# Attention with a gated feed-forward: when GpSimd forms the down-weight sums, who scales the query weights, and the order of the first gate/up products

## The chip, the cores and the metric

One core of a Trainium2 chip runs the whole program. The metric is the device time of one execution in microseconds (us); lower is better. The engines are TensorE (PE in the profile, PEld for its weight loads), VectorE (DVE), ScalarE (ACT), GpSimd (POOL) and SyncE (SP, which here only issues DMAs). Each engine works through its own instructions in the order in which the program issued them, and waits on semaphores.

## The reference, cut to what matters

```python
xn   = layernorm(x)                                   # x: 2048 x 512
q    = xn @ wq                                        # 32 heads of 128
s    = (softmax(q k_cache^T / sqrt(128)) v_cache) @ wo    # 2048 keys, every head
gate = xn @ W_gate ; up = xn @ W_up                   # 512 -> 1792
g    = silu((relu(gate) * up) @ W_down)               # 1792 -> 512
out  = x + s * g
```

All inputs are bfloat16. There is no mask.

## The kernel before

The 2048 rows are four blocks of 512, Q0 to Q3. The program has three stages that matter here.

**Head.** Q0 goes through gate and up in the usual way (14 chunks of 128 hidden columns) and then through the down product `emit_down`: four tiles j = 0 to 3 of 128 rows, each 14 matmuls into one PSUM bank. Behind each tile ACT takes a tanh into `sig_sb`, and DVE makes two operations (lines 866 and 870) that write the gate `g_sb`. Between the tiles the program inserts other work. DVE builds the sums of transposed rows `TX` (kept in the buffer `xn_sb`) and `TZ` (lines 642 to 665) that the next stage reads, and POOL builds the weight sums `SG` of chunks 0 and 1 (`gu_sums`, lines 684 to 689). The sums of chunk 0 lie in the buffer `PT`, those of chunk 1 in `SG`, at the same address as the second tanh buffer.

**The 768-column pass.** Gate and up of Q1, Q2 and Q3 are done as a 2 by 2 block product with seven products instead of eight, m = 1 to 7. Each product is four matmuls (two of 512 and two of 256 columns), all at line 1236. One chunk k of 14 has its seven products, `emit_gu(k, m)`, in the order 1, 2, 6, 5, 7, 4, 3, woven between two chunks by the step number 7k + off[m]. Results are carried by copies of ACT (line 1247) and additions of DVE (lines 1190 and 1243), all of which read PSUM. DVE then multiplies gate by up from SBUF operands alone: line 1180 (512 columns, into `hT`) and line 1181 (256 columns, into a small buffer in `PT` that a DMA saves). `gside(t, ...)` hangs other work on step t. At the end of the pass the first three score pairs of attention and one query product step are woven in.

**Attention.** 128 blocks (head, Q) of eight pairs each. A pair is two score matmuls (line 1705), one exponential of ACT (line 1723) and eight value matmuls (line 1820). The PSUM banks for scores and all other products are a ring of three slots of two banks; PE waits for the oldest slot to be read. Tables say after which pair of which block (block, pair) other work is issued: `at(...)` for PE products and `side` for the rest. So the query projection of the next heads (`emit_st`, line 940 on PE, lines 945 and 954 on DVE), and the down product of Q1, Q3 and Q2 as seven products `emit_d` (line 1320, then lines 1329 to 1360 on DVE) run between pairs. For Q1, `emit_d` runs m = 1, 2, 6, 5, 7, 3, 4 at (0,2), (1,5), (2,5), (3,4), (4,5), (5,0) and (5,5). It needs sums of `hT` (`emit_hs`, DVE, lines 818 to 827) and sums of the down weights (`emit_wd_sums`, four POOL operations of 1792 columns, lines 794 to 800): m = 6 waits for the second of them, m = 7 for the third, m = 4 for the fourth.

In this kernel `emit_wd_sums` is listed at pairs (0,0) to (0,3), and then POOL scales the query weights of heads 2 and 3 (line 707) and forms their sums (`emit_sw(1)`). POOL's order alone decides when they start: the sums wait only for the scaled weights, which ACT has ready by then.

Three waits matter below, in `gu_sums`, in `emit_wd_sums` and in `emit_S_tile`, where the exponential of pair 3 waits for the last of lines 1180 and 1181:

```python
if k == 1:
    _wait(pool, sem_g.cur())
...
if k == 0:
    _wait_all(pool, [wd_tok["scale"], sem_nm.cur()])
...
if gp == NPB - 3:
    _wait(act, sem_hp.cur())
```

Of the kernel before, what the change touches and what calls it, by code (L numbers as in the profile page):

```python
# [6 lines left out]
F32 = mybir.dt.float32  # L7
F16 = mybir.dt.float16
ALU = mybir.AluOpType
# [43 lines left out]
def bass_recurrent_scan__mha_block_cached__glu_gated_reglu__prompt_kernel(  # L53
# [22 lines left out]
    FC = F // 128  # L76
# [40 lines left out]
    with ExitStack() as es:  # L117
# [60 lines left out]
        gr_sb = [at_(96256 + 1024 * i, [128, NQ], BF16, "gr_sb") for i in range(NSLOT)]  # L178
        sig_sb = [at_(99328 + 2048 * i, [128, D], F32, "sig_sb") for i in range(2)]
        small = [103424]  # L180
# [496 lines left out]
        def gu_sums(k):  # L677
            W, X = w_chunk(k), SG[k % 2]
            _wait_all(pool, [gu_tok[(k, "s")], gu_tok.get((k - 2, 7))])
            if k == 1:  # L680
                _wait(pool, sem_g.cur())
            a11, a12 = W[:, 0, 0:HC, :], W[:, 0, HC:DC, :]
            a21, a22 = W[:, 1, 0:HC, :], W[:, 1, HC:DC, :]
            k1 = sem_sg.sig(pool.tensor_tensor(X[:, 0], a21, a22, ALU.add))
# [9 lines left out]
        sw_tok = {}  # L694

        def emit_sw(pr):
            b = pr % 2
            W = Wq_sb[b]
            _wait(pool, wq_tok(pr))
            if pr >= 3:  # L700
                _wait(pool, qp_done_tok[pr - 2])
            wflat = W[:].rearrange("p c i e -> p (c i e)")
            if pr == 0:
                _wait(act, wq_tok(pr))
                k = sem_tws.sig(act.activation(wflat, wflat, ACTF.Copy, scale=WSC))
            else:
                k = sem_sw.sig(pool.tensor_scalar(wflat, wflat, WSC, None, op0=ALU.mult))  # L707
# [5 lines left out]
            if pr == 1:  # L713
                _wait(pool, sem_gup.cur())
            k1 = sem_sw.sig(pool.tensor_tensor(X[:, 0], a21, a22, ALU.add))
# [69 lines left out]
        def emit_wd_sums(k):  # L785
# [48 lines left out]
        def emit_down(h_last_tok, between):  # L834
            ytok = None
            for j in range(4):
# [27 lines left out]
                _wait(dve, stok)  # L864
                ttok = sem_g.sig(
                    dve.tensor_scalar(sig_sb[jb][:], sig_sb[jb][:], 1.0, r2[:, j, 0:1],
                                      op0=ALU.add, op1=ALU.mult))
                _wait(dve, ttok)
                gtok = sem_g.sig(
                    dve.tensor_tensor(g_sb[:, n, :], sig_sb[jb][:], yps, ALU.mult))  # L870
                sig_free[jb] = gtok
                if j < 2:
                    acc_free[jb] = gtok
                else:
                    ring_tok[s] = ring_tok[s] + [gtok]
                y_last["t"] = ytok
# [325 lines left out]
        def emit_gu(k, m):  # L1202
# [953 lines left out]
        def gu_begin():  # L2156
            gpool[:] = [s_ for s_ in ring_order if s_ != ring_order[-1]] + [NSLOT, ring_order[-1]]

# [6 lines left out]
        def gu_run(a, b):  # L2165
# [129 lines left out]
```

## Time and profile before

| | us |
|---|---|
| three runs of the kernel before | 1251.51, 1250.81, 1251.87 |
| their median | 1251.51 |
| the profiled execution | 1250.87 |
| its span in the trace | 1249.6 |
| PE busy in the span | 1218.5 |
| ACT, DVE, POOL busy | 1075.5, 864.1, 783.4 |

Times in the trace count from the start of the span; about 1.3 us of the profiled execution lie outside it. In the rows of the timeline the first column is the start in us and the second the duration (where a row stands for several instructions, from the start of the first to the end of the last). Then come the engine, the line in the source, the operation, what is written and read, and the shapes. In brackets stands how long the engine was idle ahead of the instruction and who ended that. The head ends and the 768-column pass begins near 41 us; the pass ends near 127 us, where the first pairs of attention are already under way.

### The profile page before, as it was taken

To read this page: it belongs to the slowest core of one execution; us is meant where nothing else is said; L and a number is where in the kernel's file an instruction comes from. 1 tells how busy PE (TensorE), PEld (TensorE's weight loads), DVE (VectorE), ACT (ScalarE), POOL (GpSimd) and SP (SyncE) were. 2 spreads that over 40 slices of the span, in tenths; PEclk is the share of its full clock that TensorE was granted. 3 is DMA by queue.
4 is the path that set the end of the run, shared out by engine and by line. 5 is a ranking of instruction groups with operands and counts; after the bars stand their busy time and mean duration, and the time that the engine had idled before them with its cause. 6 is when DMAs were issued, how large, how long until landed. Compare 5 with 4: busy or idle time off the path is not lost.

```text
span 1249.6 us, 29220 instructions
## 1 busy us (share of the span) xinstructions
PE 1218.5 (98%) x11798; PEld 825.1 (66%) x12010; DVE 864.1 (69%) x1304; ACT 1075.5 (86%) x1154; POOL 783.4 (63%) x904
## 2 busy tenths in 40 slices
PE   9996999999999999999999999999999999999998
PEld 5453677776666666666666666666666666666665
DVE  6899635546667776667666776677766766676587
ACT  7684777878899999999999999999999999999994
POOL 3557010013567767887768867886788776758367
PEclk9997999999999999999999999999999999999999
DMA  9500144115222445237533664347522762348616
GB/s 286 98 30 22 31 90 106 31 39 127 56 52 47 94 114 165 36 64 195 172 70 52 174 161 119 52 98 178 174 36 60 186 190 52 52 102 156 128 37 138
DMA packets 273719, 127.23 MB, mean 102 GB/s; under 512 B 238768, under 2 KB 268208, under 8 KB 268720
## 3 DMA queue, kind: packets, MB, share of 16 engines
q1 hardware_dynamic: 272240, 124.55, 42.7%
q8 instruction: 96, 1.57, 0.5%
q10 hardware_dynamic: 1344, 0.79, 0.2%
q14 instruction: 39, 0.32, 0.1%
HBM read 56.10 MB, written 27.00 MB: 67 GB/s over the span
## 4 chain that ended last, share of the span: by engine, by line
PE 94%; issue 2%; DVE 2%; POOL 1%; ACT 1%; DVEq 0%; POOLq 0%; ACTq 0%
PE ps_acc L1820 37%; PE ps_r L1705 34%; PE ps_r L1076 5%; PE ps_r L1602 3%; PE ps_r L1236 3%; PE ps_r L1320 3%; PE ps_r L940 2%; PE ps_r L1537 2%; PE ps_r L773 2%; PE ps_acc L1236 1%; DVE PT L1181 1%; PE ps_r L1634 1%; PE ps_r L1633 1%; PE ps_r L855 0%; PE ps_acc L855 0%
## 5 line engine op out<-in xcount | busy, mean ns | idle before, releaser
L1723 ACT ACTIVATE PT<-ps_r 128x1024 bf16<-128x1024 f32 x1024 | 987.8, 1025 | 119.4 <-PE ps_r L1705 101.8
L1820 PEld LDWEIGHTS ps_acc<-V_sb,PT 128*128 128x128 bf16 x8192 | 547.1, 98 | 223.5 <-issue 31.0
L1820 PE MATMUL ps_acc<-V_sb,PT 128*128 128x129 bf16 x8192 | 635.6, 220 | 1.1
L1705 PE MATMUL ps_r<-QT_sb,KT_sb 128*128 128x512 bf16 x1851 | 578.6, 380 | 15.4 <-DVE gu L1243 4.4
L1081 DVE TENSOR_TENSOR UVR<-UVR,ps_r 128x512 f32<-128x512 f32 (+1 forms) x228 | 168.9, 756 | 96.7 <-PE ps_r L1076 91.9
L1705 PEld LDWEIGHTS ps_r<-QT_sb,KT_sb 128*128 128x128 bf16 x2048 | 160.5, 98 | 42.3 <-ACT PT L1723 33.8
L1468 DVE TENSOR_TENSOR s_acc<-s_acc,ps_r 128x1024 f32<-128x1024 f32 x108 | 131.5, 1220 | 27.3 <-PE ps_r L1537 19.4
L1484 DVE TENSOR_TENSOR s_acc<-s_acc,ps_r 128x512 f32<-128x512 f32 x152 | 101.0, 683 | 28.9 <-PE ps_r L1602 23.5
L1743 DVE TENSOR_TENSOR Onorm<-ps_acc,rz_sb 128x512 bf16<-128x512 f32 x127 | 87.8, 691 | 4.4
L1568 POOL TENSOR_TENSOR TI<-OX 128x512 f16<-128x512 f16 x38 | 43.1, 1156 | 70.1 <-issue 68.7
L707 POOL TENSOR_SCALAR Wq_sb<-Wq_sb 128x1024 bf16<-128x1024 bf16 x3 | 8.3, 2779 | 120.1 <-DMA Wq_sb<-in_A_wq_dram 120.1
L1041 POOL TENSOR_TENSOR TI<-xn_sb 128x512 f16<-128x512 f16 x48 | 55.8, 1162 | 41.7 <-PE ps_r L1076 41.7
L1081 DVE TENSOR_TENSOR QT_sb<-UVR,ps_r 128x512 bf16<-128x512 f32 x72 | 49.5, 687 | 43.7 <-PE ps_r L1076 41.3
L1740 DVE RECIPROCAL rz_sb<-ps_acc 128x4 f32<-128x4 f32 x127 | 23.2, 182 | 76.6 <-PE ps_acc L1820 74.4
L1568 POOL TENSOR_TENSOR TI<-OT_store 128x512 f16<-128x512 bf16 (+1 forms) x38 | 45.7, 1223 | 29.1 <-PE ps_r L1602 21.7
L1041 POOL TENSOR_TENSOR TI<-xn_sb,TI 128x512 f16<-128x512 f16 x48 | 55.9, 1164 | 0.0
L1411 POOL TENSOR_TENSOR WX<-Wo_sb 128x512 f16<-128x512 bf16 x7 | 8.1, 1154 | 69.1 <-DVE Wo_sb L1401 42.2
L1041 POOL TENSOR_TENSOR TI<-xnT 128x512 f16<-128x512 bf16 x36 | 41.6, 1155 | 14.0 <-PE ps_r L1076 14.0
L1329 DVE TENSOR_TENSOR dbuf<-dbuf,ps_r 128x512 f32<-128x512 f32 x21 | 14.2, 687 | 50.0 <-PE ps_r L1320 50.0
L1076 PE MATMUL ps_r<-TI,SI 128*128 128x512 f16 x126 | 47.8, 380 | 0.1
L1602 PE MATMUL ps_r<-TI,SI 128*128 128x512 f16 x114 | 43.2, 379 | 0.0
L1041 POOL TENSOR_TENSOR TI<-xnT,TI 128x512 f16<-128x512 bf16 x36 | 41.5, 1153 | 0.0
(279 smaller groups left out, 1469.7 us busy)
## 6 DMA issues: line engine op xcount, KB each, us to landing
sums<-s_acc SPq DMA_DIRECT2D x20, 1024.0 KB, 5.8
s_acc<-sums SPq DMA_DIRECT2D x18, 1024.0 KB, 5.1
V_sb<-in_A_v_cache_dram SPq DMA_DIRECT2D x32, 512.0 KB, 4.5
Wq_sb<-in_A_wq_dram SPq DMA_DIRECT2D x16, 256.0 KB, 4.2
Wo_sb<-in_A_wo_dram SPq DMA_DIRECT2D x8, 512.0 KB, 3.8
out_dram<-g_sb SPq DMA_DIRECT2D x4, 512.0 KB, 4.7
KR<-sums SPq DMA_DIRECT2D x4, 512.0 KB, 4.7
OT_store<-Onorm SPq DMA_TRANSPOSE x127, 3.0
```

The costliest lines, as they stand in the source:

```text
L1041: return sem_ui.sig(pool.tensor_tensor(dst, x, y, o))
L1076: return sem_up.sig(pe.matmul(dst, lhs, rhs, start=start, stop=stop, skip_group_check=True))
L1081: dve.tensor_tensor(dst, x, ps, ALU.add))
L1236: ins = pe.matmul(ps(s)[:, a * NQ:a * NQ + (NX if a else NQ)], L(i), r, start=start and i == 0, stop=stop and i == HC - 1, skip_group_chec ...
L1468: t = sem_opa.sig(dve.tensor_copy(dst, sb) if new[0] else dve.tensor_tensor(dst, dst, sb, op))
L1484: t = dve.tensor_tensor(dst, dst, sb, op)
L1568: return sem_oi.sig(pool.tensor_tensor(dst, x, y, o))
L1602: return sem_op.sig(pe.matmul(dst, lhs, rhs, start=start, stop=stop, skip_group_check=True))
L1705: ins = pe.matmul(ps_r[:, 2 * s + tt, :], KT_sb[h % 2][:, t * 128:(t + 1) * 128], QT_sb[qt_slot[(h, Q)]][:], start=True, stop=True)
L1723: act.activation(PT[pb][:], ps_r[:, 2 * s:2 * s + 2, :], ACTF.Exp, scale=scale / WSC)
L1743: dve.tensor_tensor(Onorm[ob][:], o_ap, rz_sb[:].to_broadcast([128, 4, Dh]), ALU.mult))
L1820: ins = pe.matmul(o_ap, PT[pb][:, tt, j * 128:(j + 1) * 128], V_sb[vb][:, t, 0:VW], start=(t == 0 and j % 2 == 0), stop=(t == KT - 1 and j ...
```

## The change

Six edits, in the program's order:

1. The tanh buffers `sig_sb` move to the place of four query buffers (`QT_sb` 6 to 9), which are not yet used. `gu_sums(1)` on POOL then no longer waits for the gates of the head.
2. The first products come in another order. Before: m = 1 of chunk 0, ten matmuls of the last down tile, m = 6, its last four matmuls, then m = 2 and m = 5 of chunk 0 and m = 1 of chunk 1. Now: m = 1, eleven matmuls, m = 2, m = 6, the last three matmuls, m = 1 of chunk 1, then m = 5. The two DVE operations that finish tile j = 2 are issued behind those that read m = 2, and m = 6 of chunk 1 comes ahead of its m = 2.
3. The query weights of heads 2 and 3 are scaled by ACT (`scale_wq1`) at step 71 of the pass, no longer by POOL.
4. `emit_sw(1)` is issued at (0,1), ahead of the down-weight sums, and waits besides for line 1181 of the last chunk.
5. Six of the eight `emit_hs` operations of Q1 move from (1,1) to (1,4) into (0,1) to (0,3), the last two to (3,1) and (3,2).
6. The four down-weight sums are issued at (0,4), and the first waits for the sixth of those `emit_hs` operations.

```diff
-        sig_sb = [at_(99328 + 2048 * i, [128, D], F32, "sig_sb") for i in range(2)]
+        sig_sb = [at_(qt_at - base[0] + 6144 + 2048 * i, [128, D], F32, "sig_sb") for i in range(2)]
...
-            if k == 1:
-                _wait(pool, sem_g.cur())
...
+        def scale_wq1():
+            _wait(act, wq_tok(1))
+            w = Wq_sb[1][:].rearrange("p c i e -> p (c i e)")
+            wq1_tok.append(sem_wds.sig(act.activation(w, w, ACTF.Copy, scale=WSC)))
...
+            elif pr == 1:
+                k = wq1_tok[0]
...
             if pr == 1:
-                _wait(pool, sem_gup.cur())
+                _wait_all(pool, [sem_gup.cur(), gu_tok["f", 1, FC - 1]])
...
             if k == 0:
-                _wait_all(pool, [wd_tok["scale"], sem_nm.cur()])
+                _wait_all(pool, [wd_tok["scale"], sem_nm.cur(), hs_tok[(1, 1, 2)]])
...
-                    if fc == 10 and (j, "mid") in between:
+                    if fc == 11 and (j, "mid") in between:
...
+                if j == 2:
+                    y_last["out"] = gate_out
                 else:
-                    ring_tok[s] = ring_tok[s] + [gtok]
+                    gate_out()
...
                 if k == 0:
-                    _wait_all(act, [h_last, sem_g.cur()])
+                    _wait(act, h_last)
...
             for i, (part, k) in enumerate(hs_seq):
-                side.setdefault(((1, 6, 11)[n], (1, 2, 2, 3, 3, 4, 4, 5)[i]), []).append((emit_hs, Q, part, k))
+                bp = ((0, 1 + i // 2) if i < 6 else (3, i - 5)) if n == 0 else ((1, 6, 11)[n], (1, 2, 2, 3, 3, 4, 4, 5)[i])
+                side.setdefault(bp, []).append((emit_hs, Q, part, k))
+            for i in range(0 if n else 4):
+                side.setdefault((0, 4), []).append((emit_wd_sums, i))
...
-        side.setdefault((0, 7), []).append((emit_sw, 1))
+        gside(71, scale_wq1)
+        side.setdefault((0, 1), []).append((emit_sw, 1))
...
-            side.setdefault((0, i), []).append((emit_wd_sums, i))
...
+        def gu_first():
+            gu_run(2, 3)
+            y_last["out"]()
+            gpool.append(ring_order[-1])
+            gu_run(3, 4)
...
-            (3, "mid"): [(gu_sums, 1), (gu_run, 3, 4)]})
-        _wait_all(dve, [y_last["t"], sem_g.cur()])
-        gu_run(1, 3)
-        gu_run(4, 7 * FC - 1)
+            (3, "mid"): [(gu_sums, 1), (gu_first,)]})
...
+        for t in (7, 4, 5, 6, 8, 10, 9):
+            gu_run(t, t + 1)
+        gu_run(11, 7 * FC - 1)
```

Three places of the programs' order show what moved; line numbers are those of the kernel that is shown. First POOL at the end of the pass, in the kernel before. `SG_87` are the weight sums of the last chunk, `WdT_57` and `Wd_38_55` the down-weight sums, `SW_82` the query-weight sums.

```order
L687 TENSOR_TENSOR SG_87<-SG_87,WGU_61 128x256
L689 TENSOR_TENSOR SG_87<-WGU_61,SG_87 128x256
L794 TENSOR_TENSOR WdT_57<-Wd_sb_54 128x1792
L796 TENSOR_TENSOR WdT_57<-Wd_sb_54,WdT_57 128x1792
L798 TENSOR_TENSOR Wd_38_55<-Wd_sb_54 128x7x256
L800 TENSOR_TENSOR WdT_57<-WdT_57,Wd_sb_54 128x1792
L707 TENSOR_SCALAR Wq_sb<-Wq_sb 128x1024
L715 TENSOR_TENSOR SW_82<-Wq_sb 128x256
```

The same place of POOL in the changed kernel:

```order
L685 TENSOR_TENSOR SG_87<-SG_87,WGU_61 128x256
L687 TENSOR_TENSOR SG_87<-WGU_61,SG_87 128x256
L723 TENSOR_TENSOR SW_82<-Wq_sb 128x256
L724 TENSOR_TENSOR SW_82<-Wq_sb 128x256
L726 TENSOR_TENSOR SW_82<-SW_82,Wq_sb 128x256
L728 TENSOR_TENSOR SW_82<-Wq_sb,SW_82 128x256
L802 TENSOR_TENSOR WdT_57<-Wd_sb_54 128x1792
L804 TENSOR_TENSOR WdT_57<-Wd_sb_54,WdT_57 128x1792
```

The four long sums stand behind the four short ones, and the scaling is gone from POOL.

Second, DVE where attention begins, in the kernel before, from the last line 1181 of the pass (`PT`) on. `dbuf` is the first down product of Q1, `HS_sb` and `hT` on the left are `emit_hs`, the other rows belong to query steps and to the normalisation of block 0.

```order
L1181 TENSOR_TENSOR PT<-gu_93,uB_96 128x256
L945 TENSOR_TENSOR Wo_sb<-Wo_sb,ps_r 128x512 x2
L1360 COPY dbuf_100<-ps_r 128x512
L945 TENSOR_TENSOR QT_sb<-Wo_sb,ps_r 128x512
L945 TENSOR_TENSOR Wo_sb<-Wo_sb,ps_r 128x512
L945 TENSOR_TENSOR QT_sb<-Wo_sb,ps_r 128x512
L1740 RECIPROCAL rz_sb_74<-ps_acc 128x4
L1743 TENSOR_TENSOR Onorm_77<-ps_acc,rz_sb_74 128x512
L945 TENSOR_TENSOR cuv_66_83<-cuv_66_83,ps_r 128x512
L945 TENSOR_TENSOR cuv_67_84<-cuv_66_83,ps_r 128x512
L818 TENSOR_TENSOR HS_sb_58<-hT_52 128x1024
```

The same place of DVE in the changed kernel:

```order
L1195 TENSOR_TENSOR PT<-gu_93,uB_96 128x256
L959 TENSOR_TENSOR Wo_sb<-Wo_sb,ps_r 128x512 x2
L826 TENSOR_TENSOR HS_sb_58<-hT_52 128x1024
L829 TENSOR_TENSOR hT_52<-hT_52 128x4x256
L1374 COPY dbuf_100<-ps_r 128x512
L832 TENSOR_TENSOR HS_sb_58<-hT_52 128x1024
L826 TENSOR_TENSOR HS_sb_58<-hT_52 128x768
L829 TENSOR_TENSOR hT_52<-hT_52 128x3x256
L832 TENSOR_TENSOR HS_sb_58<-hT_52 128x768
L959 TENSOR_TENSOR QT_sb<-Wo_sb,ps_r 128x512
```

Two of the sums of `hT` stand ahead of the copy of the first down product and four behind it; the rest of the order is kept.

Third, DVE at the end of the head, before: the last operation on `TZ`, the gates of tiles 1, 2 and 3, and the first operations of the pass.

```order
L665 TENSOR_TENSOR TZ_99<-xnT,TZ_99 128x512
L866 TENSOR_SCALAR sig_sb_66<-sig_sb_66,r_50_67 128x512
L870 TENSOR_TENSOR g_sb<-sig_sb_66,ps_acc 128x512
L866 TENSOR_SCALAR sig_sb_65<-sig_sb_65,r_50_67 128x512
L870 TENSOR_TENSOR g_sb<-sig_sb_65,ps_r 128x512
L866 TENSOR_SCALAR sig_sb_66<-sig_sb_66,r_50_67 128x512
L870 TENSOR_TENSOR g_sb<-sig_sb_66,ps_r 128x512
L1190 TENSOR_TENSOR gA_97<-ga_89,ps_r 128x768
L1200 TENSOR_SCALAR gA_97<-gA_97 128x768
L1243 TENSOR_TENSOR uB_95<-ga_88,ps_r 128x768
```

In the changed kernel:

```order
L665 TENSOR_TENSOR TZ_99<-xnT,TZ_99 128x512
L876 TENSOR_SCALAR sig_sb_66<-sig_sb_66,r_50_67 128x512
L880 TENSOR_TENSOR g_sb<-sig_sb_66,ps_acc 128x512
L1204 TENSOR_TENSOR gA_97<-ga_89,ps_r 128x768
L1214 TENSOR_SCALAR gA_97<-gA_97 128x768
L876 TENSOR_SCALAR sig_sb_65<-sig_sb_65,r_50_67 128x512
L880 TENSOR_TENSOR g_sb<-sig_sb_65,ps_r 128x512
L876 TENSOR_SCALAR sig_sb_66<-sig_sb_66,r_50_67 128x512
L880 TENSOR_TENSOR g_sb<-sig_sb_66,ps_r 128x512
L1257 TENSOR_TENSOR uB_95<-ga_88,ps_r 128x768
```

The first two operations of the pass, which read m = 2 of chunk 0, have moved ahead of the gates of tiles 2 and 3.

More of the change, by code (lines that the diff above doesn't have):

```diff
@@ L694, in bass_recurrent_scan__mha_block_cached__glu_gated_reglu__prompt_kernel @@
         sw_tok = {}
+        wq1_tok = []
+        def scale_wq1():
+            _wait(act, wq_tok(1))
+            w = Wq_sb[1][:].rearrange("p c i e -> p (c i e)")
+            wq1_tok.append(sem_wds.sig(act.activation(w, w, ACTF.Copy, scale=WSC)))
         def emit_sw(pr):
@@ L698, in emit_sw @@
             W = Wq_sb[b]
-            _wait(pool, wq_tok(pr))
+            if pr > 1:
+                _wait(pool, wq_tok(pr))
             if pr >= 3:
@@ L863, in emit_down, with gate_out @@
                     act.activation(sig_sb[jb][:], yps, ACTF.Tanh, scale=r2h[:, j, 0:1]))
[L864 to L873, printed above, removed]
+                def gate_out(j=j, n=n, jb=jb, yps=yps, s=s if j > 1 else None, stok=stok):
+                    _wait(dve, stok)
+                    ttok = sem_g.sig(
+                        dve.tensor_scalar(sig_sb[jb][:], sig_sb[jb][:], 1.0, r2[:, j, 0:1],
+                                          op0=ALU.add, op1=ALU.mult))
+                    _wait(dve, ttok)
+                    gtok = sem_g.sig(
+                        dve.tensor_tensor(g_sb[:, n, :], sig_sb[jb][:], yps, ALU.mult))
+                    sig_free[jb] = gtok
+                    if j < 2:
+                        acc_free[jb] = gtok
+                    else:
+                        ring_tok[s] = ring_tok[s] + [gtok]
+                if j == 2:
+                    y_last["out"] = gate_out
                 else:
-                    ring_tok[s] = ring_tok[s] + [gtok]
+                    gate_out()
                 y_last["t"] = ytok
@@ L2156, in gu_begin @@
         def gu_begin():
-            gpool[:] = [s_ for s_ in ring_order if s_ != ring_order[-1]] + [NSLOT, ring_order[-1]]
+            gpool[:] = [s_ for s_ in ring_order if s_ != ring_order[-1]] + [NSLOT]
+        def gu_first():
[3 more added lines that the diff above has]
+            gu_run(3, 4)
         def gu_end():
@@ L2177, in bass_recurrent_scan__mha_block_cached__glu_gated_reglu__prompt_kernel @@
             2: [(gu_begin,), (gu_run, 0, 1)],
-            (3, "mid"): [(gu_sums, 1), (gu_run, 3, 4)]})
-        _wait_all(dve, [y_last["t"], sem_g.cur()])
-        gu_run(1, 3)
-        gu_run(4, 7 * FC - 1)
+            (3, "mid"): [(gu_sums, 1), (gu_first,)]})
+        for i, (slot, tok) in enumerate(qt_free):
+            if 6 <= slot < 10:
+                qt_free[i] = (slot, sem_g.cur())
+        for t in (7, 4, 5, 6, 8, 10, 9):
+            gu_run(t, t + 1)
+        gu_run(11, 7 * FC - 1)
         gu_end()
```

## The prediction

> **What bounds the kernel now.** I read the page first, for the chain that ended last, then a table of stretches, for where PE has holes, then the timeline of the worst hole, engine by engine, and last the places to which work is moved.
>
> The chain by engine, and four stretches (length, then busy time of PE, PEld, DVE, ACT and POOL, then the granted clock):
>
> ```profile
> PE 94%; issue 2%; DVE 2%; POOL 1%; ACT 1%; DVEq 0%; POOLq 0%; ACTq 0%
> 75.00:85.00 10.00, 9.94 (x62) 5.68 (x62) 9.62 (x20) 8.27 (x11) 5.59 (x9) 1.00 0.09 29
> 85.00:95.00 10.00, 9.94 (x62) 5.70 (x61) 9.62 (x20) 6.53 (x9) 5.71 (x9) 1.00 0.08 26
> 105.00:125.00 20.00, 9.55 (x36) 4.20 (x36) 18.75 (x14) 5.07 (x7) 16.61 (x5) 0.68 0.04 13
> 140.00:150.00 10.00, 9.90 (x100) 7.12 (x100) 8.07 (x15) 8.07 (x10) 0.00 (x0) 1.00 0.07 16
> ```
>
> PE is the bound nearly everywhere: 9.94 of 10 us in the pass, 9.90 in attention. So time that PE gains or loses at one place should reach the end. The exception is 105 to 125, where PE has 9.55 of 20 us, and part of that at a clock of 0.68. DVE is busy for 18.75 us there with 14 instructions and POOL for 16.61 with five. The timeline of that hole:
>
> ```profile
> 104.35 3.57 POOL L794 TENSOR_TENSOR WdT<-Wd_sb 128x1792 f16<-128x1792 bf16 x1
> 104.69 3.51 DVE L1180 TENSOR_TENSOR hT<-gA,gu 128x512 f16<-128x512 bf16 x1
> 108.12 3.65 DVE L1181 TENSOR_TENSOR PT<-gA,gu 128x256 f16<-128x256 bf16 x1
> 111.58 3.62 POOL L798 TENSOR_TENSOR Wd<-Wd_sb 128x1792 f16<-128x1792 bf16 x1
> 111.69 0.94 DVE L1243 TENSOR_TENSOR uB<-ga,ps_r 128x768 bf16<-128x768 f32 x1
> 112.69 0.61 PE L1236 MATMUL ps_r<-xn_sb,WGU 128*128 128x512 f16 x1 [5.85 <-DVE uB L1243]
> 115.16 3.74 POOL L800 TENSOR_TENSOR WdT<-WdT,Wd_sb 128x1792 f16<-128x1792 f16 x1
> 115.41 3.65 DVE L1181 TENSOR_TENSOR PT<-gu,uB 128x256 f16<-128x256 bf16 x1
> 121.08 1.03 PE L1705 MATMUL ps_r<-QT_sb,KT_sb 128*128 128x512 bf16 x2 [4.37 <-DVE gu L1243]
> 100.12 0.42 DVE L1180 TENSOR_TENSOR hT<-gA,gu 128x512 f16<-128x512 bf16 x1
> 100.47 0.28 DVE L1181 TENSOR_TENSOR PT<-gA,gu 128x256 f16<-128x256 bf16 x1
> ```
>
> One step earlier lines 1180 and 1181 took 0.42 and 0.28. Beside a down-weight sum of POOL they take 3.51 to 3.65, and each ends 0.2 us after that sum. Both read two SBUF operands. In the middle of the third sum line 1243, which reads one operand from PSUM, takes 0.94 and is done at 112.63, long before that sum ends at 115.2. So a long POOL operation shuts out the first kind and not the second. Three such waits delay DVE's line 1243, for which PE stands 5.85 and 4.37 us, and the matmul behind has 0.61 instead of 0.38.
>
> **The long sums leave the pass (edits 4 and 6).** POOL has nothing between the last weight sum and line 1181 of the last chunk, so lines 1180 and 1181 go back to 0.42 and 0.28. I rebuild the stretch from the end of m = 6 of chunk 13 to the first down product of Q1, with the durations of undisturbed rows:
>
> ```profile
> 102.11 0.38 PE L1236 MATMUL ps_r<-xn_sb,WGU 128*128 128x512 f16 x1
> 102.76 0.81 PE L1236 MATMUL ps_r<-xnT,SG 128*128 128x512 bf16 x4
> 106.57 0.27 PE L1236 MATMUL ps_acc<-TZ,SG 128*128 128x256 f16 x1
> 127.15 0.59 PE L1705 MATMUL ps_r<-QT_sb,KT_sb 128*128 128x512 bf16 x2
> 127.58 1.03 PE L940 MATMUL ps_r<-xn_sb,Wo_sb 128*128 128x512 f16 x4
> 128.45 0.62 PE L1820 MATMUL ps_acc<-V_sb,PT 128*128 128x129 bf16 x8
> 130.67 1.02 ACT L1723 ACTIVATE PT<-ps_r 128x1024 bf16<-128x1024 f32 x1 [2.50 <-DVE PT L1181]
> 131.97 0.38 PE L1705 MATMUL ps_r<-QT_sb,KT_sb 128*128 128x512 bf16 x1 [2.02 <-ACT PT L1723]
> 132.19 1.69 PE L1320 MATMUL ps_r<-Wd_sb,hT 128*128 128x256 bf16 x14
> ```
>
> From start to start a product of the pass costs 0.65 (102.11 to 102.76), a score pair 0.43, a query step 0.87. Between 106.68 (0.11 after the last matmul of m = 6 starts) and 132.19 stand six products, 3.9; five score pairs, 2.15; two query steps, 1.74; and two pairs of value matmuls with the rest, 1.3: 9.1 us of PE at full clock, in 25.5 elapsed. Not all 16.4 come back, since the tail of the pass is a chain through ACT and DVE (0.05 us from one engine to the next, as from 112.63 to 112.69). Followed through: m = 4 follows m = 6 at once, as in the step before (102.11, with no idle time in brackets), then m = 3 and m = 5; the second score pair waits for the line 1243 that reads m = 4, ahead of which DVE has one more 1243, 1190, 1180, 1181 and 1200 (from about 105.6 to 109.1; 0.5 lost); the query step waits for the first exponential (0.4); and the exponential of pair 3 waits for the last line 1181, now near 115.0, ends near 116.1, and releases the fifth score pair. The down product then starts near 116.6. **Gain: 132.2 - 116.6 = 15.6 us**, of which the two holes are 10.2, the hole of 2.02 shrinks by 1.8, and the rest is clock. Ends: 16.4 (no wait at all) and 10.2 (the two holes alone).
>
> **What hides the moved work.**
>
> ```profile
> 127.47 0.67 POOL L715 TENSOR_TENSOR SW<-Wq_sb 128x256 f16<-128x256 bf16 x1 [5.78 <-PE ps_acc L1236]
> 127.69 0.72 DVE L1180 TENSOR_TENSOR hT<-gA,gu 128x512 f16<-128x512 bf16 x1
> 129.82 0.75 DVE L1181 TENSOR_TENSOR PT<-gu,uB 128x256 f16<-128x256 bf16 x1
> 133.92 0.69 DVE L1360 COPY dbuf<-ps_r 128x512 f32<-128x512 f32 x1 [1.96 <-PE ps_r L1320]
> 137.00 0.69 DVE L945 TENSOR_TENSOR QT_sb<-Wo_sb,ps_r 128x512 bf16<-128x512 f32 x1 [2.40 <-PE ps_r L940]
> 141.92 0.69 DVE L818 TENSOR_TENSOR HS_sb<-hT 128x1024 f16<-128x1024 f16 x1
> 145.15 0.56 DVE L824 TENSOR_TENSOR HS_sb<-hT 128x768 f16<-128x768 f16 x1
> 155.51 1.69 PE L1320 MATMUL ps_r<-WdT,HS_sb 128*128 128x256 f16 x14
> L1743 DVE TENSOR_TENSOR Onorm<-ps_acc,rz_sb 128x512 bf16<-128x512 f32 x127 | 87.8, 691 | 4.4
> ```
>
> The short sums of the query weights fell on the last four operations 1180 and 1181 (the first and last shown). Those took 0.72, 0.75, 0.88 and 0.75 instead of 0.42 and 0.28 twice: 1.7 us on the way to pair 3's exponential. Now the sums wait for the last 1181, and fall on the first `emit_hs` operations. The six of those (0.69 three times, 0.56 three times, from 141.92 to 145.71) go into DVE's two idle spells, two into the 1.96 ahead of the copy and four (2.4 us) into the 2.40 behind it. Nothing waits there but the copy, at worst 0.7 late, and a ring slot that PE wants three pairs later. Cost 0, upper end 1.
>
> The long sums then start near 137.0 - 15.6 = 121.4 and end near 136 (four of 3.6). PE's m = 6 of Q1, which needs the second of them (128.7), stands at 155.5 - 15.6 = 139.9: 11 us to spare; m = 7 and m = 4 come one and three blocks later. POOL has nothing else queued there. DVE's operations in that time are query steps, normalisations and down combinations, all with an operand from PSUM. Line 1743 keeps a mean of 691 ns over 127 blocks, while POOL is busy for 783.4 of 1249.6 us. Cost 0. If that cover fails, it is the second rival. The last two `emit_hs` come after the sums.
>
> **The scaling on ACT (edit 3)** adds one ACT operation to the pass. In 75 to 85 ACT scales down-weight chunks of the same size and has 8.27 us of work in eleven operations; in 85 to 95 it has 6.53 in nine, so one such costs 0.9. PE has 9.94 in both stretches. Cost 0, upper end 0.9; below nothing there is no reason for a gain but that POOL loses an operation, which no engine waits for in the pass.
>
> **The first products (edits 1, 2).** This is where I expect a loss.
>
> ```profile
> 40.35 1.00 DVE L642 TENSOR_TENSOR xn_sb<-xnT 128x1024 f16<-128x1024 bf16 x1 [0.59 <-DMA xnT<-xn_sb]
> 41.28 0.68 DVE L644 TENSOR_TENSOR xn_sb<-xnT 128x1024 f16<-128x1024 bf16 x1
> 44.33 0.42 DVE L665 TENSOR_TENSOR TZ<-xnT,TZ 128x512 f16<-128x512 bf16 x1
> 44.85 0.38 PE L1236 MATMUL ps_r<-xn_sb,PT 128*128 128x512 f16 x1 [0.77 <-issue]
> 47.13 0.67 POOL L684 TENSOR_TENSOR SG<-WGU 128x256 f16<-128x256 bf16 x1 [6.32 <-DVE g_sb L870]
> 51.22 0.38 PE L1236 MATMUL ps_r<-xn_sb,WGU 128*128 128x512 f16 x1
> ```
>
> POOL stood 6.32 us for a gate before the sums of chunk 1. Without that wait it goes on at 40.8, into the eight operations of DVE from 642 to 665, all from SBUF. The first of them met the last operation of chunk 0 and took 1.00 instead of 0.68. Four short sums among such operations cost DVE 1.7 us at 127.47. Here the operations are longer, and in turn they give about 2.0: `TZ` is ready near 46.8 instead of 44.75. PE's m = 6, which began at 44.85, waits for it; the new order puts m = 2 (0.65) in front, so PE stands from 44.75 to 46.8. From there the chain is DVE's: gate of tile 1 (1.1 us, as before), 1190 and 1200 (1.3), gates of tiles 2 and 3 (about 2.3, and 0.3 more beside the sums of chunk 2), 1243 (0.95), so m = 4 of chunk 0 starts near 52.7 instead of 51.22: **a loss of 1.5 us**. Ends: with no contention the same chain starts at 44.75 and gives 50.4, a gain of 0.8; with every short sum paid in full beside the longest operation, a loss of 2. I take 1.5, by the four rows at 127.47.
>
> The Trainium skill (SBUF — State Buffer, Who interferes with whom) calls the port pair of VectorE and GpSimd an exclusive lock that the first to issue holds for its whole instruction. It adds that two SBUF inputs contend and one does not. By that each of the four sums could cost DVE its whole 0.67, 2.7 in all, and the sum below would be 0.7 worse; the rows give less, since part of a DVE operation lies outside the wait.
>
> **Sum.** -15.6 + 1.5 + 0 + 0 = -14.1, against the profiled 1250.87: 1236.8. The median of the runs lies 0.64 above the profiled one, so I predict 1237.4.
>
> **Rivals.**
> 1. *A new wait at the start of attention.* The chain above was followed by hand through three engines, and the ring leaves PE two pairs of slack. One more missed slot, or the `emit_hs` operations pushing the copy and the query step late, costs one to two exponentials or one query step more, 2 to 5 us: 1239.5 to 1242.5. For it: DVE has 0.1 us to spare in its second idle spell. Against it: PE needs none of these results for three pairs.
> 2. *The lock moves with the sums; slower.* If operations with a PSUM operand were held too, each of the four sums would hold one of DVE's combinations for 3.6 us at 121 to 136, 14.5 in all, and PE would stop when its three slots are full, with a cold clock as now. That takes back 14.5 and about 1.7 of clock: -15.6 + 16.2 + 1.5 = +2.1, 1253.6. It decides as soon as a combination such as 945 shows 3.5 us. Against it: the 0.94 at 111.69, and the 691.
> 3. *No contention at `TZ`.* If DVE wins the race at 40.8, POOL waits and edits 1 and 2 gain 0.8: -16.4, 1235.1. Against it: 1.00 in the row at 40.35.
> 4. *Only the holes go.* The chain of the tail keeps its pace and 10.2 + 1.8 comes back: -12.0 + 1.5, 1241.0. That would need another late producer in the tail; the rows show none.
>
> **How the numbers follow.** The forecast 0.68 (1235.8 to 1239), the first rival 0.13, the second 0.03, the third 0.10, the fourth 0.06. The range 1234.8 to 1241.5 takes the forecast, the third, the fourth and most of the first. Faster by over 0.2% (2.5 us, about what a measurement of this kernel can tell from no change): 0.96; within it 0.02; slower 0.02.
>
> **What would show it.** In the new profile lines 1194 and 1195 (old 1180, 1181) keep 0.42 and 0.28 through the last chunk; PE has no hole over 1 us from the end of the pass to the first down product, at clock 1.00; the four long sums stand about 5 us behind that product, and DVE's combinations beside them keep 0.69. At the head, POOL's second set of sums starts at 40.8, lines 642 to 665 end near 46.8, and PE has a hole of 2 us in front of m = 6. I am wrong if a combination beside a long sum takes 3.5 us, if a PE hole of several us stands in block 0, or if `TZ` is not late.

## The result, and the profile after

| | before | after |
|---|---|---|
| median of the runs, us | 1251.16 (1250.58 to 1251.87, 4 runs) | 1236.06 (1235.29 to 1236.40, 4 runs) |
| ratio, with its 95% interval | | 0.9878 (0.9861 to 0.9895) |
| profiled execution, us | 1250.87 | 1235.98 |
| its span, us | 1249.6 | 1234.7 |

The changed kernel is 1.2% faster. The forecast was 1237.4 with a range of 1234.8 to 1241.5; it lay 1.3 us too high. The span, 14.9 us shorter, can be cut at four PE rows that both kernels have. The first product of the pass is m = 1 of chunk 0. Its row before was this one of the timeline:

```profile
41.11 0.81 PE L1236 MATMUL ps_r<-xnT,WGU 128*128 128x512 bf16 x4
```

| stretch, us | before | after | difference | forecast |
|---|---|---|---|---|
| start to first product of the pass | 41.11 | 40.74 | -0.37 | 0 |
| from there to m = 4 of chunk 0 | 10.11 | 10.96 | +0.85 | +1.5 |
| from there to m = 6 of chunk 13 | 54.81 | 54.80 | -0.01 | 0 |
| from there to the first down product of Q1 | 26.16 | 10.61 | -15.55 | -15.6 |
| the rest | 1117.4 | 1117.6 | +0.2 | 0 |

The change leaves PE's order ahead of the pass's first product as it was. That product started between 40.60 and 41.29 in the profiles of this study, so -0.37 is within the spread of that place. To keep this spread out, the experiments below use M, the time from the first product of the pass to the start of the first down product of Q1: 91.08 before, 76.37 after. M repeats closely: the changed kernel profiled again gave 76.42.

First the chain that ended last, by engine, on the page of the changed kernel:

```profile
PE 94%; issue 2%; POOL 1%; DVE 1%; ACT 1%; DMA 0%; DVEq 0%; POOLq 0%; ACTq 0%
```

PE carries it as before. DVE's share was 2% and is 1%. Then three stretches of the same kernel (length, then busy time of PE, PEld, DVE, ACT and POOL, then the granted clock); the last runs from m = 6 of chunk 13 to the first down product.

```profile
105.00:125.00 20.00, 19.31 (x151) 11.89 (x152) 17.89 (x35) 14.62 (x17) 6.42 (x5) 1.00 0.19 51
125.00:135.00 10.00, 9.89 (x100) 7.12 (x100) 3.42 (x7) 8.07 (x10) 9.92 (x4) 1.00 0.07 15
106.50:117.11 10.61, 9.97 (x65) 5.34 (x65) 10.10 (x21) 7.00 (x8) 1.45 (x3) 1.00 0.11 37
```

Where PE had 9.55 of 20 us at a clock of 0.68, it has 19.31 at 1.00. The next stretch, 125 to 135, is where the long sums now lie: POOL has 9.92 of 10 us, and PE still 9.89. The timeline of the tail, engine by engine:

```profile
105.16 0.42 DVE L1194 TENSOR_TENSOR hT<-gA,gu 128x512 f16<-128x512 bf16 x1
105.51 0.28 DVE L1195 TENSOR_TENSOR PT<-gA,gu 128x256 f16<-128x256 bf16 x1
115.21 0.28 DVE L1195 TENSOR_TENSOR PT<-gu,uB 128x256 f16<-128x256 bf16 x1
115.59 1.02 ACT L1737 ACTIVATE PT<-ps_r 128x1024 bf16<-128x1024 f32 x1 [0.79 <-DVE PT L1195]
115.67 0.67 POOL L723 TENSOR_TENSOR SW<-Wq_sb 128x256 f16<-128x256 bf16 x1 [10.81 <-DVE PT L1195]
116.89 0.38 PE L1719 MATMUL ps_r<-QT_sb,KT_sb 128*128 128x512 bf16 x1 [0.31 <-ACT PT L1737]
117.11 1.69 PE L1334 MATMUL ps_r<-Wd_sb,hT 128*128 128x256 bf16 x14
118.84 0.69 DVE L1374 COPY dbuf<-ps_r 128x512 f32<-128x512 f32 x1 [0.25 <-PE ps_r L1334]
121.92 0.69 DVE L959 TENSOR_TENSOR QT_sb<-Wo_sb,ps_r 128x512 bf16<-128x512 f32 x1
121.95 3.59 POOL L802 TENSOR_TENSOR WdT<-Wd_sb 128x1792 f16<-128x1792 bf16 x1 [2.83 <-DVE HS_sb L832]
124.80 0.69 DVE L1757 TENSOR_TENSOR Onorm<-ps_acc,rz_sb 128x512 bf16<-128x512 f32 x1
132.70 3.57 POOL L808 TENSOR_TENSOR WdT<-WdT,Wd_sb 128x1792 f16<-128x1792 f16 x1
140.43 1.69 PE L1334 MATMUL ps_r<-WdT,HS_sb 128*128 128x256 f16 x14
```

Lines 1194 and 1195 (old 1180 and 1181) keep 0.42 and 0.28 to the last chunk. The score pair ahead of the first down product waits 0.31 instead of 2.02. The short sums start after the last 1195. The first and the last of the four long sums are shown; the two DVE rows between them, beside the first sum, take 0.69, as when POOL is idle.

At the head, POOL's second set of weight sums and the DVE operations that lead to `TZ`, in the same timeline:

```profile
40.40 1.11 POOL L682 TENSOR_TENSOR SG<-WGU 128x256 f16<-128x256 bf16 x1
40.74 0.81 PE L1250 MATMUL ps_r<-xnT,WGU 128*128 128x512 bf16 x4
40.91 1.16 DVE L644 TENSOR_TENSOR xn_sb<-xnT 128x1024 f16<-128x1024 bf16 x1
43.75 1.00 POOL L687 TENSOR_TENSOR SG<-WGU,SG 128x256 f16<-128x256 bf16 x1
45.73 0.43 DVE L665 TENSOR_TENSOR TZ<-xnT,TZ 128x512 f16<-128x512 bf16 x1
46.26 0.38 PE L1250 MATMUL ps_r<-xn_sb,PT 128*128 128x512 f16 x1 [1.68 <-issue]
51.70 0.39 PE L1250 MATMUL ps_r<-xn_sb,WGU 128*128 128x512 f16 x1
```

POOL and DVE stretch each other: the sums take 1.00 to 1.11 (0.67 alone) and line 644 takes 1.16 (0.68). `TZ` is ready 5.42 us after the first product instead of 3.64, and PE stands 1.68 us in front of m = 6. Part of that comes back before m = 4 (last row).

### The profile page after: what moved, and what is told of

Read it like the earlier page. It is cut to its first block, busy times and chain, and to the rows that moved or that the text cites. A ratio compares the mean times of both kernels' runs of the same rounds, so it can differ in the third digit from the quotient of the medians.

```text
span 1234.7 us, 29217 instructions
## 1 busy us (share of the span) xinstructions
PE 1214.5 (98%) x11798; PEld 823.5 (67%) x12010; DVE 851.3 (69%) x1304; ACT 1076.1 (87%) x1155; POOL 781.5 (63%) x903
## 4 chain that ended last, share of the span: by engine, by line
PE 94%; issue 2%; POOL 1%; DVE 1%; ACT 1%; DMA 0%; DVEq 0%; POOLq 0%; ACTq 0%
PE ps_acc L1834 37%; PE ps_r L1719 34%; PE ps_r L1090 5%; PE ps_r L1250 3%; PE ps_r L1616 3%; PE ps_r L1334 3%; PE ps_r L954 2%; PE ps_r L1551 2%; PE ps_r L781 2%; PE ps_acc L1250 1%; ACT PT L1737 1%; PE ps_r L1648 1%; PE ps_r L1647 1%; DMA xnT<-xn_sb 0%; PE ps_r L513 0%
## 5 line engine op out<-in xcount | busy, mean ns | idle before, releaser
L715 POOL TENSOR_SCALAR Wq_sb<-Wq_sb 128x1024 bf16<-128x1024 bf16 x2 | 5.5, 2770 | 99.6 <-DMA Wq_sb<-in_A_wq_dram 99.6
```

## The experiments

**Theory.** The gain comes only from the four long sums being out of the way of DVE's operations with two SBUF operands at the end of the pass. Edits 1 and 2 lose about 1 us, and edits 3 and 5 do nothing by themselves. **Rivals.** The first products earn part of the gain; the scaling's move to ACT earns it; the earlier `emit_hs` operations do; or the length of a single POOL operation matters, not its place.

### The changed kernel once more, and its two halves

The first two of these runs are the changed kernel itself and a kernel with edits 1 and 2 alone:

```diff
-        side.setdefault((0, 1), []).append((emit_sw, 1))
+        side.setdefault((0, 7), []).append((emit_sw, 1))
...
+            side.setdefault((0, i), []).append((emit_wd_sums, i))
...
```

> The changed kernel once more, beside its variants on the same chip. Expected 1236.1 us (+-0.7).

> Edits 1 and 2 alone (tanh buffers moved, first products in another order, POOL's second weight sums early); the long sums stay in the pass. Theory: POOL's early sums hold back TZ, PE gets the fourth product of chunk 0 about 0.85 us later (10.96 us after the first product instead of 10.11), so about 1252.0 us, +0.5 to +1.3 against before. Rival (the new order itself gains and the loss lies elsewhere): 1250 us or less.

Measured: the changed kernel 1236.28 against 1250.48, ratio 0.9887 (0.9874 to 0.9901), M 76.42. Edits 1 and 2 alone: 1251.42, ratio 1.0008 (0.9999 to 1.0016), M 92.28, which is 1.20 more than before. PE's waits from 100 to 175 in the latter (us in total, times, the longest):

```profile
PE ps_r L1240 <- DVE uB L1247: 5.9, 1, 5.9
PE ps_r L1709 <- DVE gu L1247: 4.1, 1, 4.1
PE ps_r L1709 <- ACT PT L1727: 2.0, 1, 2.0
```

The three holes of the kernel before are all there. At the head, 10.99 us lie between the first product and m = 4 of chunk 0, as in the changed kernel (10.96). So the first products earn nothing. By the rows they cost 0.9; by the medians 0.9 too, with an interval that reaches from no change to 2 us.

The other half, edits 3 to 6 alone, keeps the old first products:

```diff
-            (3, "mid"): [(gu_sums, 1), (gu_first,)]})
+            (3, "mid"): [(gu_sums, 1), (gu_run, 3, 4)]})
...
```

> Edits 3 to 6 alone (long sums held, query weights scaled on ACT, sums of hT early); the first products as before. Theory: the whole gain of 15.5 us at the end of the pass and no loss at its start, so 1235.3 us, 0.5 to 1.3 below the changed kernel. Rival (part of the gain comes from the head): 1237 us or more.

Measured: 1235.77, ratio 0.9881 (0.9867 to 0.9894), M 75.30. That is 15.8 below before and 1.1 below the changed kernel. The medians of the two do not differ by more than their spread; the rows of its timeline at the head do, m = 6 and m = 4 of chunk 0:

```profile
44.38 0.38 PE L1249 MATMUL ps_r<-xn_sb,PT 128*128 128x512 f16 x1 [0.53 <-issue]
50.75 0.38 PE L1249 MATMUL ps_r<-xn_sb,WGU 128*128 128x512 f16 x1
```

PE waits 0.53 instead of 1.68 for `TZ`, and m = 4 of chunk 0 starts 9.87 after the first product instead of 10.96. The profiles of this study bear that out: this time is 10.87 to 11.00 in the seven with edits 1 and 2 as they stand, and 9.87 to 10.37 in the three without them.

### The sums of chunk 1 held until TZ is done

The changed kernel, with one wait on POOL:

```diff
+            if k == 1:
+                _wait(pool, tx_tok["z"])
```

> The changed kernel, but POOL's sums of chunk 1 wait for the last operation on TZ. Theory: the eight DVE operations take 0.68 and 0.42 again, PE's hole of 1.68 us ahead of m = 6 goes, m = 4 of chunk 0 starts about 9.4 to 9.7 us after the first product instead of 10.96, so 1234.6 us, 1.3 to 1.6 below the changed kernel. Rival (the hole has another cause, or the sums of chunk 1 come too late for m = 6 of chunk 1): within 0.4 us of the changed kernel.

Measured: 1235.72, ratio 0.9883 (0.9868 to 0.9898), M 75.38; m = 4 starts 9.93 after the first product, outside the expected 9.4 to 9.7. Its timeline, from the last `TZ` operation to m = 4:

```profile
43.99 0.43 DVE L665 TENSOR_TENSOR TZ<-xnT,TZ 128x512 f16<-128x512 bf16 x1
44.52 0.38 PE L1252 MATMUL ps_r<-xn_sb,PT 128*128 128x512 f16 x1
46.74 0.89 DVE L878 TENSOR_SCALAR sig_sb<-sig_sb,r 128x512 f32<-128x512 f32 x1
49.80 0.82 PE L1252 MATMUL ps_r<-xnT,WGU 128*128 128x512 bf16 x4 [1.23 <-DVE g_sb L882]
50.66 0.39 PE L1252 MATMUL ps_r<-xn_sb,WGU 128*128 128x512 f16 x1
```

`TZ` is early again (3.6 us after the first product) and the hole in front of m = 6 is gone. But a new one of 1.23 us stands in front of m = 2 of chunk 1, behind the gate of tile 3 (`g_sb`), which DVE runs last of the gates. The contention at `TZ` is the cause of the loss; without it, edits 1 and 2 still earn nothing over the kernel that lacks them (M 75.38 against 75.30), since the gates are the next thing that is late. POOL's short sums, put off, now fall on these gates: line 878 takes 0.89 for tile 2 and, at 48.27, 0.76 for tile 3, instead of 0.48. These 0.7 us stand in the chain to m = 4, which misses the expected start by 0.2 to 0.5. No run keeps the gates clear as well.

### The sums issued without the wait for emit_hs

```diff
-                _wait_all(pool, [wd_tok["scale"], sem_nm.cur(), hs_tok[(1, 1, 2)]])
+                _wait_all(pool, [wd_tok["scale"], sem_nm.cur()])
```

> The changed kernel, but the long sums do not wait for the sums of hT: they start behind POOL's short sums, near 119 us, while four operations on hT still stand ahead of the query step on DVE. Theory (a long POOL operation holds any DVE operation with two SBUF operands): each of the four takes about 3.6 us, the query step behind them is some 11 us late, PE stops when its three slots are full; 1244 to 1249 us. Rival (the exclusion matters in the pass only): 1237 us or less.

Measured: 1250.76, ratio 1.0001 (0.9992 to 1.0011). The whole gain is lost, more than the expected upper end. Its timeline (start, length, engine, line, operation, and in brackets the idle time ahead and who ended it):

```profile
119.53 3.57 POOL L802 TENSOR_TENSOR WdT<-Wd_sb 128x1792 f16<-128x1792 bf16 x1
119.91 3.75 DVE L832 TENSOR_TENSOR HS_sb<-hT 128x1024 f16<-128x1024 f16 x1
123.58 3.92 DVE L826 TENSOR_TENSOR HS_sb<-hT 128x768 f16<-128x768 f16 x1
131.36 3.80 DVE L832 TENSOR_TENSOR HS_sb<-hT 128x768 f16<-128x768 f16 x1
135.09 0.67 DVE L959 TENSOR_TENSOR QT_sb<-Wo_sb,ps_r 128x512 bf16<-128x512 f32 x1
137.01 1.03 PE L1719 MATMUL ps_r<-QT_sb,KT_sb 128*128 128x512 bf16 x2 [12.01 <-DVE QT_sb L959]
```

The stretch from 117 to 145 of the same run:

```profile
117.00:145.00 28.00, 15.91 (x144) 10.71 (x144) 21.76 (x15) 11.82 (x14) 17.59 (x7) 0.82 0.13 27
```

Each of four `emit_hs` operations is held for one long sum (the fourth, not shown, for 3.80). They stand ahead of a query step in DVE's order, and PE waits 12.01 us for that step, then runs at a low clock for some microseconds (the mean of the stretch is 0.82). The stretch up to the first down product is as good as in the changed kernel (M 76.28). So it is not enough that the sums leave the pass: the wait of edit 6 is needed as soon as `emit_hs` stands early.

### The emit_hs operations back in their old place

The six `emit_hs` operations return to (1,1) to (1,4), and the long sums follow them at (1,4), still behind that wait:

```diff
-                bp = ((0, 1 + i // 2) if i < 6 else (3, i - 5)) if n == 0 else ...
+                bp = ((1, (1, 2, 2, 3, 3, 4)[i]) if i < 6 else (3, i - 5)) if n == 0 else ...
...
-                side.setdefault((0, 4), []).append((emit_wd_sums, i))
+                side.setdefault((1, 4), []).append((emit_wd_sums, i))
```

> The changed kernel with the six sums of hT back in block 1 ((1,1) to (1,4)) and the long sums issued at (1,4) behind them. Theory (PE's m = 6 has about 11 us to spare, so the early place of the sums of hT earns nothing by itself): within 0.7 us of the changed kernel, 1235.6 to 1237.5, at worst 2 us more where a long sum holds the gate operation with two SBUF operands at 137 us. Rival (the early sums of hT are part of the gain): 1239 us or more.

Measured: 1236.67, ratio 0.9889 (0.9874 to 0.9904), M 76.37. Its timeline where the sums now lie:

```profile
131.15 3.58 POOL L802 TENSOR_TENSOR WdT<-Wd_sb 128x1792 f16<-128x1792 bf16 x1 [12.47 <-DVE HS_sb L832]
137.02 1.91 DVE L1356 SCALAR_TENSOR_TENSOR g_sb<-dbuf,dbuf 128x512 bf16<-128x512 f32 x1
140.87 0.59 PE L1719 MATMUL ps_r<-QT_sb,KT_sb 128*128 128x512 bf16 x2 [0.35 <-DVE QT_sb L959]
```

The earlier place of `emit_hs` is no source of the gain; what counts is that the long sums and `emit_hs` do not lie beside each other, and the order with its wait sees to that. The sums now start 9 us later and meet one other operation with two SBUF operands, line 1356, which takes 1.91 (0.68 in the changed kernel); PE waits 0.35 for it.

### The scaling back on POOL

Edit 3 undone, all else kept:

```diff
-            if pr > 1:
-                _wait(pool, wq_tok(pr))
+            _wait(pool, wq_tok(pr))
...
-            elif pr == 1:
-                k = wq1_tok[0]
...
-        gside(71, scale_wq1)
```

> The changed kernel with the query weights of heads 2 and 3 scaled by POOL again; it then does so right behind the last weight sums, near 105 us, in the tail of the pass. Theory: one POOL operation of 2.8 us holds one or two DVE operations there, +0.3 to +2.5 us, 1236.5 to 1238.7. Rival (the scaling on ACT is worth nothing): 1236.1.

Measured: 1236.59, ratio 0.9887 (0.9872 to 0.9902), M 76.50, 0.1 above the changed kernel. I had expected 0.3 to 2.5. The median lies at the lower edge of that and cannot tell it from the rival, nothing; M speaks for the rival. Its timeline at the end of the pass:

```profile
104.97 2.77 POOL L712 TENSOR_SCALAR Wq_sb<-Wq_sb 128x1024 bf16<-128x1024 bf16 x1
105.31 0.98 DVE L1191 TENSOR_TENSOR hT<-gA,gu 128x512 f16<-128x512 bf16 x1
106.21 0.28 DVE L1192 TENSOR_TENSOR PT<-gA,gu 128x256 f16<-128x256 bf16 x1
```

The POOL operation runs from 104.97 to 107.74. Line 1191 in it takes 0.98 instead of 0.42, and line 1192 right behind takes its 0.28. So this POOL operation, with one SBUF operand, does not hold DVE to its end as the long sums, with two, do.

The place matters here too. In the kernel before, the scaling stood behind the long sums, in the chain of the second hole:

```profile
118.88 2.80 POOL L707 TENSOR_SCALAR Wq_sb<-Wq_sb 128x1024 bf16<-128x1024 bf16 x1
118.98 1.18 DVE L1200 TENSOR_SCALAR gA<-gA 128x768 bf16<-128x768 bf16 x1
```

Line 1200 takes 0.35 elsewhere in the pass and 1.18 here, and the line 1243 for which PE stood 4.37 us comes right behind it. So about 0.8 us of that hole belonged to the scaling, by the rows; the run above puts it where DVE has time to spare and does not test this.

### The long sums cut into seven, in their old place

The kernel before, with each sum of 1792 columns made of seven operations of 256:

```diff
-                t = pool.tensor_tensor(WdT[:, 0], b12, b11, ALU.subtract)
...
+            for i in range(HF):
+                t = pool.tensor_tensor(dst[:, i], x[:, i], y[:, i], ALU.subtract)
```

> The kernel before, but each of the four long sums is cut into seven operations of 256 columns, at the same place. POOL's work grows from 14.5 to about 17.4 us. Theory (a POOL operation holds one DVE operation, for as long as it itself takes): nine DVE operations of the tail lose about 0.4 us each instead of 3.3, PE's two holes shrink from 10.2 us to 1 to 3, 1238 to 1242 us. Rival (POOL's total time beside the pass counts): 1250 us or more.

Measured: 1239.09, ratio 0.9908 (0.9891 to 0.9924), M 80.00 in its profiled run, 11.1 less than before. Its timeline:

```profile
104.39 4.90 POOL L796 TENSOR_TENSOR WdT<-Wd_sb 128x256 f16<-128x256 bf16 x7
105.26 0.75 DVE L1179 TENSOR_TENSOR PT<-gA,gu 128x256 f16<-128x256 bf16 x1
120.39 0.71 PE L1703 MATMUL ps_r<-QT_sb,KT_sb 128*128 128x512 bf16 x2 [2.16 <-ACT PT L1721]
120.89 3.19 PE L1318 MATMUL ps_r<-Wd_sb,hT 128*128 128x256 bf16 x14
```

The stretch of the last two rows:

```profile
120.39:124.00 3.61, 3.61 (x18) 2.46 (x19) 0.21 (x1) 1.94 (x2) 3.61 (x6) 0.55 0.70 160
```

The same sums among the same DVE operations hold them 0.75 instead of 3.65, and three quarters of the gain (11.1 of 14.7 in M) are there without any move. Not all of it is due to the shorter operations: the four sums take 19.1 us instead of 14.5, so the scaling behind them now falls after the pass (123.49). What M lacks against the changed kernel is in the main a hole of 2.16 us and two of about 1 us. Another 1.5 us lie behind the end of M, in the first down product (3.19 instead of 1.69, at a clock of 0.55). They belong to this execution: the other three of the kernel took 1238.91 to 1239.12, against 1240.64 for this one.

### The query-weight sums without their wait

```diff
-                _wait_all(pool, [sem_gup.cur(), gu_tok["f", 1, FC - 1]])
+                _wait(pool, sem_gup.cur())
```

> The changed kernel without the wait of POOL's query-weight sums for the last line 1195: they start when PE ends the pass, near 114 us, beside the last four operations 1194 and 1195. Theory: those four take 0.72 to 0.88 again, 1.7 us in all, the exponential of pair 3 and PE's slot come that much later (PE hole near 2 us instead of 0.31), +1.0 to +1.7 us, 1237.1 to 1237.8. Rival (that wait is worth nothing): 1236.1, holes as in the changed kernel.

Measured: 1237.56 against 1250.97, ratio 0.9886 (0.9872 to 0.9901), M 78.15, 1.8 more than in the changed kernel. Its timeline ahead of the first down product:

```profile
114.45 0.67 POOL L723 TENSOR_TENSOR SW<-Wq_sb 128x256 f16<-128x256 bf16 x1 [9.24 <-PE ps_acc L1250]
116.81 0.75 DVE L1195 TENSOR_TENSOR PT<-gu,uB 128x256 f16<-128x256 bf16 x1
118.95 0.38 PE L1719 MATMUL ps_r<-QT_sb,KT_sb 128*128 128x512 bf16 x1 [2.02 <-ACT PT L1737]
```

The short sums are back on the last four operations 1194 and 1195, and the hole of 2.02 us is back with them. The added wait of edit 4 is worth 1.8 of the 15.6.

### A version that takes the first products further

The run with `TZ` left the gate of tile 3 as the next late step. This kernel keeps that wait and puts the gate behind line 1259 (1257 in the changed kernel) of chunk 0 on DVE:

```diff
+            if k == 1:
+                _wait(pool, tx_tok["z"])
...
-                if j == 2:
-                    y_last["out"] = gate_out
+                if j >= 2:
+                    y_last["out", j] = gate_out
...
+        for t in (7, 4, 5, 6, 8):
+            gu_run(t, t + 1)
+        y_last["out", 3]()
...
-        for t in (7, 4, 5, 6, 8, 10, 9):
+        for t in (10, 11, 12, 13, 9):
             gu_run(t, t + 1)
-        gu_run(11, 7 * FC - 1)
+        gu_run(14, 7 * FC - 1)
```

> A version meant to beat both: the changed kernel, POOL's sums of chunk 1 wait for TZ, the gate of tile 3 is issued behind line 1257 of chunk 0 on DVE, and m = 4, 3 of chunk 0 and m = 5 of chunk 1 run ahead of m = 2 of chunk 1, which needs the bank of that tile. Theory (what is left of PE's holes at the head is DVE's chain of gates, 1.23 us ahead of m = 2 of chunk 1): that hole goes, m = 1 of chunk 2 starts near 10.8 us after the first product instead of 12.1, 1234.2 to 1235.0. Rival (DVE is the bound there in any order): 1235.7, m = 1 of chunk 2 after 12.1 us.

Measured: 1234.55 (1234.25 to 1235.19), ratio 0.9865 (0.9848 to 0.9881), M 74.64, 1.7 below the changed kernel. Its timeline, m = 4 of chunk 0 and m = 2 of chunk 1 with what follows it:

```profile
49.69 0.39 PE L1252 MATMUL ps_r<-xn_sb,WGU 128*128 128x512 f16 x1 [0.74 <-DVE uB L1259]
51.65 1.46 PE L1252 MATMUL ps_r<-xnT,WGU 128*128 128x512 bf16 x7
```

m = 4 of chunk 0 now starts 8.56 after the first product and waits 0.74 for its own producer, and m = 2 of chunk 1 no longer waits for a gate. m = 1 of chunk 2 starts about 11.2 after the first product, later than the expected 10.8 and earlier than the rival's 12.1. It is the fastest kernel of the study. Its ratio's interval overlaps that of the changed kernel, so it is M that says it is faster, and by how much.

## Why the prediction was right, point by point

**The bound and the main term.** -15.6 was forecast between m = 6 of chunk 13 and the first down product, -15.55 measured. The steps hold too: counted from m = 6, the exponential of pair 3 was to end after 10.1 us (116.1 less 106.03) and did (116.61 less 106.50), and PE was to be idle for about 1 us there and was for 0.64 (9.97 busy of 10.61). The split into causes is shown in part: 1.8 for the short sums (the run without their wait). The rest goes with edits 3 to 6, since with edits 1 and 2 alone the holes stay, and with the other four alone they go. Of it about 0.8 is the scaling's by the rows (line 1200), and the long sums have what remains, some 13, by subtraction.

**Two SBUF operands, or one from PSUM.** That only the first kind is shut out was read from the 0.94 at 111.69 and a mean of 691 ns. For these two kinds it is borne out in both directions. Combinations beside the long sums keep 0.69, and the same sums hold four `emit_hs` operations for 3.75 to 3.92 as soon as they meet them. The prediction did not ask about a third kind, operations with a single tensor that comes from SBUF. They are held too: line 1200 (1.18 instead of 0.35) beside the scaling, line 878 (0.89 and 0.76 instead of 0.48) beside short sums. The Trainium skill (SBUF — State Buffer, Who interferes with whom) says the same of two SBUF inputs. That one input does not contend it says only outside certain fast modes, which `tensor_scalar` can enter; the prediction's sentence leaves this out. The rows of lines 1200 and 878 would fit it, but the trace does not show the mode. The Trainium skill adds that the engine that issues first keeps the port for its whole instruction: the long sums agree (3.51 to 3.92 beside 3.57 to 3.90), while the scaling on POOL does not (0.98, then 0.28, within 2.77). There the measurement decides. With that the second rival, 1253.6, falls for this kernel. But the run without the wait for `emit_hs` lost the whole gain (1250.76) much as that rival has it, with the hold moving along with the sums until PE stops, only on DVE operations with two SBUF operands and not on the combinations.

**The moved work.** Cost 0, as forecast. The six `emit_hs` operations lie in 116.80 to 121.78, the copy of the first down product starts 1.73 us after that product as before (133.92 less 132.19; 118.84 less 117.11), and m = 6 of Q1 stands at 140.43, 23.3 us behind the first down product as before. The first rival (a new wait, 2 to 5 us) did not occur: PE's longest wait from 104 to 175 is 0.31 us. The fourth rival (only the holes go) falls with the 15.55.

**The scaling.** Cost 0: it takes 1.08 on ACT where 0.9 was reckoned, and PE does not wait for it. The run that puts it back on POOL, at 105, differs by 0.1 in M. The prediction saw no reason for a gain, since no engine waits for that operation; it passed over line 1200, which stood beside it in the kernel before and lost 0.8 us on the way to the second hole. That gain was in the 15.6 all the same, because the sum was reckoned from the durations of undisturbed rows.

**The first products: the term that was mis-sized.** The prediction put +1.5 and the rows show +0.85 in the profile, +0.87 and +0.88 in the first two experiments, which have that order too (all against the one profile of the kernel before; the three profiles with the old order spread by 0.5). The mechanism is the one named: POOL's early sums fall among the operations that lead to `TZ`, which is 1.78 late (forecast 2.05). What failed is the rest of the chain: the 0.3 for the sums of chunk 2 beside the gates. Those sums started at 49.82, and the gate operations before and after them took 0.48 and 0.69, their durations before. From `TZ` to m = 4 it then took 5.5 us instead of the 5.9 that I added up.

The third rival had its size wrong as well. It gave a gain of 0.8 over the kernel before if the sums kept clear of `TZ`. With that arranged, m = 4 starts 0.2 earlier than before (9.93 against 10.11), and the same as without edits 1 and 2 at all (9.87). For this rival the prediction took the gates at their undisturbed lengths. Sums that keep clear of `TZ` fall on the gates instead, and cost them 0.7 there. The prediction also followed the chain only to m = 4; the hole that replaced the old one stands at m = 2 of chunk 1, in front of it in the new order.

**The sum.** The forecast was 1.3 too high. 0.8 of it shows in the profile: the mis-sized term gives 0.65, and 0.37 is the spread of the start, which is luck, less 0.2 in the rest. The other 0.55 comes from the 0.64 added for the distance of the median from the profiled execution, which is 0.08 in the changed kernel.

**What is not settled.** The medians of the changed kernel with and without edits 1 and 2 (1236.28, 1235.77) differ by less than either spread, so their cost of about 1 us rests on the rows of the profiles, seven against three. The 0.8 of the scaling was read from rows and not tested alone. The clock of 0.55 in the run with the split sums is seen in the one execution that was profiled; the times and mean clocks of the other three speak against it there, and its cause is open.

## What to carry to other kernels

A long GpSimd operation costs VectorE nothing while VectorE's operations have an operand in PSUM, and what is left of its own length for each one that reads two from SBUF (3.5 to 3.9 us here, in place of 0.3 to 0.7). Ask of each such operation what the other engine does beside it; then place it where those operations are not on the way to a matmul, order it behind them with a wait, or cut it (seven pieces gave three quarters of the gain in the old place). A wait taken away lets an engine run ahead into another's critical chain: follow where the freed work lands, and what is late next, before counting the wait as a gain.

## What the hardware showed that was not expected

- A POOL operation with one SBUF operand holds DVE only in part: 0.98 instead of 0.42 for the first DVE operation in its 2.77 us, and 0.28 undisturbed for the next. In the kernel before it was the same: 1.18 instead of 0.35 for the first, and 0.42 undisturbed at 121.06, still within the 2.80.
- A DVE operation with one tensor, from SBUF, is held as well: 0.76 to 0.89 instead of 0.48 beside POOL sums of 0.67.
- Two short operations delay each other by turns. Four POOL sums of 0.67 took 1.00 to 1.11, DVE's operations beside them up to 1.16 (0.68), and the delay of `TZ` was 1.78 us, less than 4 times 0.67.
- The clock fell once behind holes of PE that are all short. In the profiled execution with the split sums, holes of 0.93, 1.05 and 2.16 within 10 us came ahead of a stretch at 0.55, with 3.19 us for 14 matmuls that take 1.69. A hole of 2.02 us alone, in the kernel before and in the run without the short sums' wait, was followed by matmuls at full pace. That the number of holes is the reason is not shown: the other three executions with the split sums were 1.5 us or more shorter, at a mean clock of 0.999 to 1.000 against 0.998. The Trainium skill (TensorE: Matmul & The Clock Gate, What's actually happening) names an idle window of about 3.4 us for the slow clock; none of these holes is that long.
